# A 941-operation state-space and gated-linear kernel on one core: the hand-written order replaced by another, with 14 bank evacuations on the other engine

## The chip, the cores and the metric

One core of a Trainium2 chip. The number to be judged is the device time of the whole kernel in microseconds (us), as the median of several runs. Engines are called as in the profile: PE is TensorE's matmul, PEld its weight load, DVE is VectorE, ACT is ScalarE, POOL is GpSimd, SP is SyncE, whose queue here only issues DMAs.

## The reference, cut to what matters

```python
xn = _layernorm(x)                                  # x: (1, 2048, 512), bf16
return x + _A_ref(xn, ...) + _B_ref(xn, w_gate, w_up, w_down)

def _A_ref(u, ...):                                 # a state-space layer, N = 128 states
    dB, logdA = dt * Bc, dt * A
    P = jnp.exp(logdA[:, :, None] * l[None, None, :])       # powers, l = 0..2047
    K = jnp.einsum("dn,dnl,dn->dl", Cc, P, dB).real         # one kernel per channel
    y = irfft(rfft(pad(u)) * rfft(pad(K)))[:, :L]           # causal convolution along l
    return y + u * Dskip

def _B_ref(x, w_gate, w_up, w_down):                # F = 1792
    h = _sigmoid(x @ w_gate) * (x @ w_up)
    return h @ w_down
```

## The kernel before, in words

The program first collects 941 small operations in a `_Plan`: each has an engine (or a DMA queue), a function that issues its instructions, the operations that it depends on, and the buffer slots that it takes and gives back. The list `ORDER` is then replayed by `run`. It fixes three things at once: the order of the instructions on every engine, the order of the transfers on every queue (SP's, ACT's, POOL's), and which of the buffers of a pool an operation gets, as the pools are handed out first in, first out. There is nothing dynamic after that. An engine works strictly in its order, so an instruction that waits holds all behind it. The pools that matter: `s` (two pairs of PSUM banks), `gu` (four PSUM banks), `es` (three buffers of the table E), `xx` (three of spectra), `zx`, `kb`, `pp`, `pq`, `vs` (two or more each of the convolution's stages), `hT` (eight of hidden rows), `us` (two of evacuated up rows), `ot` (three of outgoing rows).

The stages, which overlap:

- **Start.** Tiles of x are loaded, normalised (statistics at L547 and L548, the apply at L555 on ACT or L560 on DVE) and transposed on PE (L571) or by DMA (L584). Meanwhile PE runs dummy matmuls (`keep_warm`, L526): 14, 6, 3 and 3.
- **GLU.** Tokens are in four groups of 512, the hidden dimension in 14 tiles of 128. For each: gate matmuls (L1031), sigmoid on ACT (L1043), up matmuls (L1055), product on DVE (L1070). Where the tile's number 14 x group + tile stands in `UEV`, ACT first copies the up bank to `us_sb` (L1066) and DVE multiplies from there; otherwise DVE reads the bank. The down projection (L1099) makes 16 tiles of 128 tokens; tiles 0 to 11 come in between, 12 to 15 at the end.
- **Ladder and tables.** Powers on DVE (L679, L681), squares on ACT (L672), casts on either (L664 on DVE, L666 on ACT, two instructions each). In four chunks DVE then builds table products (L737 to L743 and, with ACT's squares of L790, L795 and L796), and PE multiplies by them (two table matmuls, L821, a selection, L841). The results, copied by ACT, are the kernel's transform.
- **Convolution.** Two sets, p0 and p1, of eight units. Each loads a piece of the transformed input, transforms it on PE (L892), copies the spectrum out of PSUM (L288 on DVE or L290 on ACT), swaps halves (p0: four DMAs on SP; p1: DVE copies, L905), loads a table E (320 KB), makes the kernel's spectrum on PE (L914), multiplies on DVE (L919, L923), transforms back on PE (L936), copies out and stores to `v_scr`. The unit names p0u7 and so on are set and number.
- **Tail.** `v_scr` is read back (SP and ACT queues), closing matmuls (L995, L997), corrections (L955 to L974, which read sums that POOL makes in a block named `pre`, L712 to L716), the last four down tiles, two additions on DVE (L1010 and L1119), the stores.

`ON_DVE` lists operation numbers whose copy, cast or layernorm apply goes to DVE and not to ACT. A number in it is a position in the plan, and each says what it is by its place: 64 to 87 ladder casts, 95 to 124 layernorm applies of tiles 4 to 15, 482, 542, 566 spectrum evacuations of units of p1, 836 to 846 copies of finished down tiles.

Some operation numbers that the steps below speak of: 686 and 688 are the up matmuls and the product of group 1, tile 1; 463 and 464 are the evacuation and the store of p0u6's result; 468 to 471 the four swaps and 475 the first product of p0u7; 349 the first table matmul of the last chunk; 922, 925, 929 and 934 with 936 the down tiles 12 to 15; 840, 848, 762, 754, 676 and 668 closing blocks of the tail; 167 is `pre`; 19 to 22 the dummy matmuls (14, 6, 3, 3).

Of the kernel before, what the change touches and what calls it, by code (L numbers as in the profile page):

```python
# [180 lines left out]
def _consts():  # L181
# [19 lines left out]
    return dict(SR=f(sr), ident=f(np.eye(128)), S1=f(np.tile(S1, (4, 1))), S2=f(np.stack([_build_S2(by), np.roll(_build_S2(by), 32, axis=1)], axis=1)), M2=f(quads(M2[by])), SW=f(sw),  # L201
                MAB=f(np.stack([quads(MA[by], True), quads(MB[by], True)], axis=2)), E=f(_build_E(M2, by).reshape(128, NU // 2, 2, NKT, 128).transpose(1, 0, 2, 3, 4)))

UEV = (3, 5, 8, 9, 10, 11, 15, 16, 17, 18, 19, 20, 21, 23, 24, 26, 27, 28, 29, 30, 31, 32, 33, 34, 35, 36, 37, 38, 39, 40, 41, 42, 43, 44, 45, 54)
ON_DVE = (64, 67, 73, 76, 97, 98, 110, 121, 122, 123, 124, 482, 836, 838)
ON_ACT = (2,)
ORDER = [
# [41 lines left out]

class _Op:  # L250
    __slots__ = ("alt", "tab", "eng", "cost", "fn", "prio", "acq", "rel", "dma", "left", "users", "ready", "start", "done", "seq", "mode")
# [8 lines left out]
class _Plan:  # L260
# [20 lines left out]
    def copy(self, nc, cost, out, in_, *args, **kw):  # L281

        get = lambda v: v() if callable(v) else v
        dve = len(self.ops) in ON_DVE

# [35 lines left out]
def kernel(  # L321
# [214 lines left out]
    def layernorm(i0, i1, prio):  # L536
# [14 lines left out]
        for i in range(i0, i1):  # L551
            dve = i < LN_ACT or len(pl.ops) in ON_DVE
            if not dve:
# [107 lines left out]
    def f_cast(cur, k, dve):  # L661
        for p in range(NP):
            if dve:
                V.tensor_copy(out=W[p][:, k], in_=cur[:, :, DW * p:DW * p + DW])  # L664
            else:
                S.activation(out=W[p][:, k], in_=cur[:, :, DW * p:DW * p + DW], func=ACT.Identity)  # L666
    cast_prev = [None, None]
    for k in range(12):
        cur = wt[(2 * k) % 3]
        sq, nxt = wt[(2 * k + 1) % 3], wt[(2 * k + 2) % 3]  # L670
        if k < 11:
            s_op = pl.add("ACT", 0.95, lambda cur=cur, sq=sq: S.activation(out=sq, in_=cur, func=ACT.Square),  # L672
                          [cur_op] + W_op[-1:], PLAD + k * 0.01)
        dve = len(pl.ops) in ON_DVE
        c_op = pl.add("DVE" if dve else "ACT", 1.04, lambda cur=cur, k=k, dve=dve: f_cast(cur, k, dve), [cur_op],
# [339 lines left out]
    for grp in range(4):  # L1015
        hts, prods = [], []
        for u2 in range(7):
# [4 lines left out]
            for k in (2 * u2, 2 * u2 + 1):  # L1022
# [38 lines left out]
                us = _Slot("us")  # L1061
                on = un in UEV

# [131 lines left out]
```

## Time and profile before

| | |
|---|---|
| runs | 222.93, 221.24, 221.66 us; median 221.66 |
| profiled execution | span 219.8 us, first to last activity, 1.9 below the median of the runs (the only time of that execution that is recorded) |
| busy | PE 209.2 us (95%), DVE 202.2 (92%), ACT 175.9 (80%), POOL 22.6 (10%) |
| transfers | 41.36 MB, 188 GB/s on average |
| chain that ended last, by engine | DVE 48%, PE 41%, DMA 4%, ACT 4%, issue 2% |

The profile lists busy time per engine, the span in 40 slices, the DMA queues, and the chain of work that ended last, followed back from the final instruction to what released each step. Two further views count: groups of instructions of one line and form, with busy time, the mean duration of one in ns, and the idle time before them with what ended it; and the timeline. A busy engine is not always at its peak: matmuls are pipelined, and the durations shown include the overlap with the next.

### The profile page before, as it was taken

How to read it: one execution, taken by the hardware profiler on the slowest of the kernel's cores; microseconds unless marked ns; L12 is line 12 of the kernel's file. 1: busy time of each engine (PE TensorE's matmuls, PEld its weight loads, DVE VectorE, ACT ScalarE, POOL GpSimd, SP SyncE). 2: the span in 40 equal slices, each digit the busy share in tenths (PEclk: the TensorE clock that was granted, in tenths of full speed). 3: DMA queues.
4: the chain of work that ended last, by engine and by line, in shares of the span. 5: the costliest groups of instructions: out<-in, count | busy, mean ns of one | idle time of the engine just before them, and what ended most of it. 6: DMA issues, size and time to landing. Idle time of an engine off the chain costs nothing.

```text
span 219.8 us, 5357 instructions
## 1 busy us (share of the span) xinstructions
PE 209.2 (95%) x2075; PEld 105.0 (48%) x2103; DVE 202.2 (92%) x444; ACT 175.9 (80%) x283; POOL 22.6 (10%) x39
## 2 busy tenths in 40 slices
PE   7999988999999999999999999999989999999994
PEld 2544433444434454445555555554555455543453
DVE  3999999999999999999999999999989999993582
ACT  3699999999999999769899999977578978942000
POOL 2216001001000049100000004000020100000000
PEclk9999999999999999999999999999999999999999
DMA  5997069216667064526818579856857987688743
GB/s 172 333 425 298 7 180 317 80 42 143 237 134 206 18 198 97 202 82 178 244 55 237 152 244 210 212 173 169 228 111 236 265 265 232 189 234 209 220 158 136
DMA packets 40651, 41.36 MB, mean 188 GB/s; under 512 B 9009, under 2 KB 31922, under 8 KB 40498
## 3 DMA queue, kind: packets, MB, share of 16 engines
q1 hardware_dynamic: 39458, 39.12, 57.7%
q0 software_dynamic: 864, 1.57, 4.9%
q10 hardware_dynamic: 304, 0.33, 0.6%
q8 instruction: 16, 0.26, 0.5%
q14 instruction: 9, 0.07, 0.1%
HBM read 25.28 MB, written 12.06 MB: 170 GB/s over the span
## 4 chain that ended last, share of the span: by engine, by line
DVE 48%; PE 41%; DMA 4%; ACT 4%; issue 2%; POOL 0%; DVEq 0%; ACTq 0%
PE bank L1099 11%; DVE big L738 7%; PE pair L914 7%; DVE big L737 6%; PE bank L1031 6%; PE bank L1055 6%; DVE hT_sb L1070 6%; PE pair L936 5%; DVE stats L547 4%; DVE big L742 4%; DVE big L743 3%; DVE big L679 3%; DVE big L681 3%; DMA big<-c_E 3%; ACT big L290 3%; DVE big L613 2%
## 5 line engine op out<-in xcount | busy, mean ns | idle before, releaser
L290 ACT ACTIVATE big<-pair 128x1024 bf16<-128x1024 f32 (+2 forms) x75 | 73.4, 996 | 9.2 <-PE pair L936 1.9
L1055 PE MATMUL bank<-xnT,wu_sb 128*128 128x512 bf16 x214 | 54.4, 379 | 2.5 <-ACT us_sb L1066 1.3
L1031 PE MATMUL bank<-xnT,wg_sb 128*128 128x512 bf16 (+1 forms) x211 | 50.9, 367 | 1.4 <-ACT xnT L576 0.4
L1099 PE MATMUL bank<-wd_sb,hT_sb 128*128 128x512 bf16 (+1 forms) x230 | 50.2, 366 | 0.4
L1043 ACT ACTIVATE hT_sb<-bank 128x512 bf16<-128x512 f32 x52 | 32.1, 643 | 3.8 <-PE bank L1031 3.6
L1031 PEld LDWEIGHTS <-wg_sb 128*128 128x128 bf16 x236 | 21.9, 98 | 26.4 <-issue 5.2
L1099 PEld LDWEIGHTS <-hT_sb 128*128 128x128 bf16 x238 | 22.5, 98 | 24.8 <-issue 2.1
L1055 PEld LDWEIGHTS <-wu_sb 128*128 128x128 bf16 x224 | 21.0, 97 | 27.2 <-issue 5.4
L737 DVE TENSOR_TENSOR big<-big 128x1024 bf16<-128x1024 bf16 (+4 forms) x40 | 26.8, 670 | 0.1
L738 DVE TENSOR_TENSOR big<-big 128x1024 bf16<-128x1024 bf16 (+4 forms) x40 | 26.6, 666 | 0.0
L1066 ACT ACTIVATE us_sb<-bank 128x512 bf16<-128x512 f32 x36 | 22.4, 634 | 0.0
L919 DVE TENSOR_TENSOR big<-big 128x2048 bf16<-128x2048 bf16 x16 | 19.5, 1219 | 0.4
L914 PE MATMUL pair<-big 128*128 128x256 bf16 x160 | 19.8, 272 | 0.1
L914 PEld LDWEIGHTS <-big 128*128 128x128 bf16 x160 | 15.5, 98 | 4.9 <-issue 1.1
L790 ACT ACTIVATE sq_sb<-big 128x256 bf16<-128x256 bf16 (+2 forms) x20 | 13.7, 685 | 3.9 <-DVE big L743 3.8
L743 DVE TENSOR_TENSOR big<-big 128x512 bf16<-128x512 bf16 (+4 forms) x40 | 16.6, 414 | 0.0
L742 DVE TENSOR_TENSOR big<-big 128x512 bf16<-128x512 bf16 (+4 forms) x40 | 16.5, 413 | 0.0
L290 ACT ACTIVATE big<-big 128x256 bf16<-128x256 bf16 x36 | 15.7, 470 | 0.2
L1070 DVE TENSOR_TENSOR hT_sb<-hT_sb,us_sb 128x512 bf16<-128x512 bf16 x36 | 14.9, 421 | 0.0
L905 DVE COPY big<-big 32x1024 bf16<-32x1024 bf16 x32 | 13.5, 421 | 0.5
L1070 DVE TENSOR_TENSOR hT_sb<-hT_sb,bank 128x512 bf16<-128x512 bf16 x20 | 13.2, 684 | 0.5 <-PE bank L1055 0.5
L936 PE MATMUL pair<-big 64*64 64x512 bf16 (+1 forms) x256 | 12.8, 326 | 0.5 <-ACT big L290 0.2
(103 smaller groups left out, 222.2 us busy)
## 6 DMA issues: line engine op xcount, KB each, us to landing
big<-c_E SPq DMA_DIRECT2D x16, 320.0 KB, 4.4
z_scr<-big SPq DMA_DIRECT2D x16, 256.0 KB, 3.0
big<-z_scr SPq DMA_DIRECT2D x16, 256.0 KB, 3.5
v_scr<-big SPq DMA_DIRECT2D x16, 256.0 KB, 2.9
big<-in_A_u_dram SPq DMA_DIRECT2D x4, 512.0 KB, 8.5
big<-big SPq DMA_DIRECT2D x32, 64.0 KB, 3.1
big<-v_scr SPq DMA_DIRECT2D x4, 512.0 KB, 5.0
wu_sb<-in_B_w_up_dram SPq DMA_DIRECT2D x2, 896.0 KB
```

What stands on the lines that cost most here:

```text
L290: nc.scalar.activation(out=get(out), in_=get(in_), func=ACT.Identity)
L737: V.tensor_tensor(out=wide(outp), in0=wide(lo), in1=mre, op=ALU.mult)
L738: V.tensor_tensor(out=wide(tb()), in0=wide(lo), in1=mim, op=ALU.mult)
L742: V.tensor_tensor(out=outp[:, :, 0], in0=outp[:, :, 0], in1=tb()[:, :, 1], op=opr)
L743: V.tensor_tensor(out=outp[:, :, 1], in0=outp[:, :, 1], in1=tb()[:, :, 0], op=opi)
L914: T.matmul(two(sk)[:, o:o + DW], es()[:, g, kt, :], kT[p][:, kt, :], start=kt in (0, NKT - 1), stop=kt >= NKT - 2)
L936: T.matmul(two(sv)[o:o + 64, DW * (2 * g + y):2 * DW * (g + 1)], mab[b:b + 64, 2 * u + g, q, :], pq()[b:b + 64, q, ch] if y else pp()[b:b ...
L1031: T.matmul(bank(sl, k % 2)[:, c0:c1], w_at(w, CUT_G, kt, k), xnT[:, grp, kt, c0:c1], start=(kt == 0), stop=(kt == KT - 1))
L1043: S.activation(out=hT_sb[:, hs.idx, k % 2, :], in_=bank(sl), func=ACT.Sigmoid)
L1055: T.matmul(bank(sl), w_at(wu_sb, CUT_U, kt, k), xnT[:, grp, kt, :], start=(kt == 0), stop=(kt == KT - 1))
L1070: V.tensor_tensor(out=h(), in0=h(), in1=us_sb[:, us.idx, :] if on else bank(sl), op=ALU.mult)
L1099: T.matmul(bank(po)[:, 0:c[1] - c[0]], hT_sb[:, hts[k // 2].idx, k % 2, jj * 128:(jj + 1) * 128], wd_sb[:, k, c[0]:c[1]], start=first and ...
```

## The change

The diff touches three constants. `UEV` goes from 36 to 35 tiles: out 5, 8, 9, 15, 19, 23, 45, in 6, 7, 25, 47, 48, 52. `ON_DVE` goes from 14 to 15: out 64, 67, 73, 76 (casts), 121, 123, 124 (applies), 482 (a spectrum), 836 (a down tile); in 82 (a cast), 95, 96, 108, 109, 111 (applies), 542, 566 (spectra), 844, 846 (down tiles). `ORDER` holds the same 941 numbers in another order. Dependencies, sizes, transfers and buffers are as they were, but which buffer of a pool an operation gets follows the new order. Of the dummy matmuls, the last two groups of three (21, 22) now stand behind the last down tile. The loads of x tiles 4 to 7 come ahead of the first gate weights, and `pre` stands at the end of POOL's queue.

```diff
--- before
+++ after
-UEV = (3, 5, 8, 9, 10, 11, 15, 16, 17, 18, 19, 20, 21, 23, 24, 26, 27, 28, 29, 30, 31, 32, 33, 34, 35, 36, 37, 38, 39, 40, 41, 42, 43, 44, 45, 54)
-ON_DVE = (64, 67, 73, 76, 97, 98, 110, 121, 122, 123, 124, 482, 836, 838)
+UEV = (3, 6, 7, 10, 11, 16, 17, 18, 20, 21, 24, 25, 26, 27, 28, 29, 30, 31, 32, 33, 34, 35, 36, 37, 38, 39, 40, 41, 42, 43, 44, 47, 48, 52, 54,)
+ON_DVE = (82, 95, 96, 97, 98, 108, 109, 110, 111, 122, 542, 566, 838, 844, 846,)
 ON_ACT = (2,)
 ORDER = [
-    1, 24, 0, 23, 2, 34, 25, 27, 4, 3, 6, 26, 33, 35, 37, 28, 36, 29, 30, 38, 43, 44, 46, 39, 40, 45, 10, 7, 13, 19,
-    20, 31, 32, 21, 41, 48, 42, 22, 592, 604, 593, 605, 615, 618, 624, 47, 90, 88, 91, 49, 11, 103, 5, 14, 104, 89,
-    606, 50, 102, 92, 93, 12, 627, 653, 658, 9, 633, 54, 594, 654, 55, 634, 610, 655, 101, 656, 106, 598, 611, 659,
...
-    721, 740, 722, 724, 674, 679, 152, 197, 81, 82, 725, 680, 198, 173, 83, 723, 199, 713, 729, 684, 730, 686, 734,
-    736, 737, 183, 112, 113, 685, 126, 84, 687, 200, 174, 86, 728, 201, 688, 735, 153, 154, 202, 689, 746, 690, 744,
...
-    164, 17, 166, 244, 138, 139, 140, 141, 375, 239, 232, 229, 262, 675, 167, 750, 751, 752, 245, 246, 212, 757, 759,
...
-    786, 769, 784, 286, 385, 293, 362, 828, 829, 463, 822, 790, 443, 823, 444, 276, 287, 386, 803, 279, 420, 440, 294,
-    824, 310, 792, 851, 852, 466, 472, 390, 365, 445, 311, 364, 464, 296, 793, 467, 387, 412, 388, 791, 787, 832, 446,
...
-    301, 363, 471, 366, 468, 405, 772, 370, 314, 474, 831, 771, 773, 302, 304, 319, 303, 305, 853, 856, 427, 394, 371,
-    327, 833, 469, 470, 475, 397, 393, 395, 389, 449, 406, 421, 328, 774, 476, 407, 320, 329, 321, 422, 834, 331, 913,
...
-    348, 424, 410, 430, 540, 845, 431, 349, 351, 838, 350, 352, 432, 565, 836, 433, 901, 404, 409, 906, 902, 415, 416,
...
-    536, 537, 897, 514, 889, 894, 515, 898, 895, 875, 576, 918, 890, 870, 876, 899, 919, 878, 538, 539, 590, 588, 582,
-    581, 577, 860, 578, 877, 591, 585, 579, 920, 900, 879, 880, 922, 840, 848, 925, 841, 842, 584, 849, 923, 926, 676,
-    668, 850, 677, 669, 678, 670, 924, 927, 929, 762, 763, 930, 933, 754, 928, 764, 755, 756, 935, 934, 936, 931, 932,
-    937, 939, 940, 938]
+    0, 1, 19, 2, 3, 4, 23, 10, 24, 6, 7, 25, 26, 33, 34, 27, 13, 11, 28, 5, 29, 43, 30, 8, 31, 35, 9, 20, 44, 37, 36, 45,
+    46, 38, 32, 39, 15, 40, 41, 47, 48, 42, 592, 12, 91, 604, 598, 88, 605, 593, 90, 49, 624, 89, 615, 101, 92, 618, 104,
+    93, 633, 50, 627, 606, 94, 634, 599, 102, 643, 619, 96, 103, 638, 594, 600, 95, 105, 625, 98, 54, 97, 51, 653, 99, 644,
...
+    174, 739, 730, 197, 705, 684, 740, 83, 686, 121, 685, 687, 706, 216, 198, 707, 688, 157, 182, 711, 84, 693, 199, 694,
...
+    294, 296, 772, 392, 420, 469, 770, 297, 463, 295, 473, 445, 771, 464, 298, 468, 398, 831, 446, 393, 474, 299, 470, 802,
+    834, 395, 399, 300, 447, 396, 803, 427, 406, 287, 448, 827, 564, 301, 276, 858, 804, 407, 475, 302, 773, 411, 304, 774,
...
+    326, 308, 343, 341, 843, 344, 342, 317, 345, 414, 346, 402, 333, 493, 403, 845, 516, 347, 494, 404, 334, 348, 415, 349,
...
+    871, 518, 355, 430, 839, 872, 569, 847, 431, 567, 358, 911, 167, 570, 556, 432, 862, 553, 571, 433, 916, 554, 876, 572,
...
+    509, 889, 884, 535, 898, 510, 536, 899, 908, 885, 511, 909, 537, 590, 873, 512, 538, 890, 874, 513, 539, 905, 875, 576,
+    514, 918, 577, 900, 893, 919, 515, 910, 587, 894, 578, 895, 920, 922, 588, 591, 585, 584, 579, 925, 581, 582, 840, 848,
+    841, 935, 923, 926, 849, 842, 762, 933, 924, 850, 754, 927, 929, 928, 763, 755, 764, 676, 756, 930, 677, 668, 934, 669,
+    678, 936, 931, 670, 937, 932, 938, 22, 939, 21, 940,]
```

53 rows, old and new, of the table ORDER are left out of this document.

## The prediction

> **What bounds the kernel now.** I read the page's first two parts, then busy time by stage, the chain that ended last, the groups by form, and last the timeline around the few places where the change could tell.
>
> ```profile
> span 219.8 us, 5357 instructions
> PE 209.2 (95%) x2075; PEld 105.0 (48%) x2103; DVE 202.2 (92%) x444; ACT 175.9 (80%) x283; POOL 22.6 (10%) x39
> ...
> 0.00:10.20 10.20, 8.60 (x42) 3.63 (x43) 6.29 (x23) 5.04 (x9) 2.52 (x12) 1.00 0.74 238
> 10.20:41.50 31.30, 28.88 (x149) 13.31 (x152) 30.61 (x71) 30.95 (x51) 5.38 (x8) 1.00 0.63 231
> 41.50:77.90 36.40, 35.84 (x185) 15.36 (x188) 36.37 (x88) 36.40 (x64) 1.07 (x1) 1.00 0.46 126
> 77.90:100.20 22.30, 22.13 (x303) 10.39 (x309) 22.16 (x55) 19.07 (x35) 8.82 (x9) 1.00 0.52 152
> 100.20:131.20 31.00, 30.30 (x393) 16.74 (x397) 31.00 (x74) 29.77 (x51) 0.36 (x2) 1.00 0.64 187
> 131.20:155.90 24.70, 24.43 (x351) 13.18 (x354) 24.67 (x53) 20.37 (x34) 2.22 (x4) 1.00 0.74 193
> 155.90:199.20 43.30, 41.85 (x558) 23.53 (x565) 40.84 (x75) 33.72 (x43) 2.26 (x3) 1.00 0.79 220
> 199.20:219.80 20.60, 17.15 (x110) 8.83 (x109) 10.23 (x12) 0.59 (x1) 0.00 (x0) 0.99 0.58 177
> ```
>
> Columns of the stages: length, then busy PE, PEld, DVE, ACT, POOL, granted clock, DMA share, GB/s. The cuts are the first gate matmul, the first down tile (41.5), the starts of the four table matmuls (L821), and tile 12 of the down projection (199.2), which opens the tail. The reader is to see that DVE is never free from 41.5 to 155.9 (114.20 of 114.40 us), that ACT is full as well in 41.5–77.9, and that PE and DVE both have about 2 us to spare only in the last long stage. So up to the fourth table matmul **DVE paces**: a wait put into its queue before 155.9 goes to the end whole. After it PE and DVE hand to each other, and the tail is PE's.
>
> **The work itself hardly changes.** The same operations run; fourteen change engine. The price of each:
>
> ```profile
> L1070 DVE TENSOR_TENSOR hT_sb<-hT_sb,us_sb 128x512 bf16<-128x512 bf16 x36 | 14.9, 421 | 0.0
> L1070 DVE TENSOR_TENSOR hT_sb<-hT_sb,bank 128x512 bf16<-128x512 bf16 x20 | 13.2, 684 | 0.5 <-PE bank L1055 0.5
> L1066 ACT ACTIVATE us_sb<-bank 128x512 bf16<-128x512 f32 x36 | 22.4, 634 | 0.0
> L666 ACT ACTIVATE big<-big 128x512 bf16<-128x512 f32 x16 | 9.8, 701 | 0.0
> L555 ACT ACTIVATE big<-big,ln_nb_f,ln_ri_f 128x512 bf16<-128x512 bf16 x5 | 4.2, 883 | 0.0
> L290 ACT ACTIVATE big<-pair 128x1024 bf16<-128x1024 f32 x63 | 64.6, 1044 | 6.3 <-PE pair L936 1.9 <-issue 1.9 <-PE pair L914 1.4
> L288 DVE CAST big<-bank 128x512 bf16<-128x512 f32 x2 | 1.3, 686 | 0.0
> L288 DVE CAST big<-pair 128x1024 bf16<-128x1024 f32 x1 | 1.2, 1225 | 0.0
> ...
> 8.42 0.65 DVE big L560 x2
> 38.91 0.67 DVE big L664 x2
> ```
>
> The last two are pieces of the chain (start, length): two layernorm applies in 0.65, two ladder casts in 0.67. On **DVE**: one product fewer has its up bank evacuated first, 0.684 − 0.421 = +0.26; four casts leave and one comes, two instructions each, 3 × −0.67 = −2.0; three layernorm applies leave and five come, 2 × 0.325 = +0.65; one spectrum evacuation leaves and two come, +1.23; one GLU copy leaves and two come, +0.69. Sum **+0.8 us**. It is not even: casts go from before 80 us, the spectrum and GLU copies come after 156, where DVE gains work worth about 0.9 and had 43.30 − 40.84 = 2.5 free. On ACT: −0.63 + 3 × 2 × 0.65 (a cast is two instructions; 0.701 overlaps a little) − 2 × 0.883 − 1.04 − 0.64 = about −0.2. On PE the sum is the same, but six dummy matmuls of L526 move from the start to after the last down tile.
>
> **The start.**
>
> ```profile
> 1.43 5.92 PE L526 MATMUL bank<-glu_sb 128*128 128x512 bf16 x20 [1.43 <-POOL glu_sb L519]
> ...
> 3.07 0.43 SPq L423 DMA_DIRECT2D wg_sb<-in_B_w_gate_dram  x1
> ...
> 3.96 0.15 PEld L526 LDWEIGHTS <-glu_sb 128*128 128x128 bf16 x1 [0.28 <-issue]
> ...
> 4.38 2.47 PEld L526 LDWEIGHTS <-glu_sb 128*128 128x128 bf16 x12 [0.27 <-issue]
> ...
> 7.49 0.72 PE L571 MATMUL pair<-ident,big 128*128 128x128 bf16 x8
> ...
> 10.20 1.03 PE L1031 MATMUL bank<-xnT,wg_sb 128*128 128x256 bf16 x8
> ```
>
> From 4.38 the weight loads of the dummies follow each other by 2.47 / 12 = 0.21 us (before it, by 0.42: 3.96 to 4.38), so the six are worth 1.3 us, and PE waited for layernorm there anyway. Against it, the load of the first gate weights is issued behind four more tiles of x. I count this even: bounds −1.3 (the dummies did hold PE up) and +0.8 (two issues of 0.43 us ahead of the weights). PE's work ahead of the first down tile is then 34.58 us against 34.66, and I leave 41.5 for it.
>
> With 14 dummies ahead of the first transposes in place of 20, seven at 0.42 and seven at 0.21, PE ends them at 5.8 and pauses 1.6 us to 7.4.
>
> [...]
>
> **41.5 to 77.9: the first new wait.** I added up the back-to-back durations of everything ahead of an instruction on its engine, in the old order and in the new one, and moved the row of the old trace by the difference.
>
> ```profile
> 63.21 1.03 PE L1055 MATMUL bank<-xnT,wu_sb 128*128 128x512 bf16 x4
> ...
> 68.92 1.26 DVE hT_sb L1070 x3
> ```
>
> The first is the up projection of group 1, tile 1; the second, in the chain, begins with its product (first instruction seen at 68.83). The new order has 5.16 us less DVE work ahead of that product, 63.67, but 0.58 more PE work ahead of the matmuls, which then end at 63.21 + 0.58 + 1.03 = 64.82. The product reads the bank itself, so DVE waits **1.2 us**; behind it stand the other products, the ladder and the table products, and ACT's squares wait for those. PE is busy 35.84 of 36.40 here, so it cannot be early. Bounds: 0 if PE comes 1.2 earlier, 1.9 if the +0.8 at the start is also there. I take 1.2.
>
> **100 to 156: the second.** In p0 the halves of a spectrum are swapped by four DMAs on SP's queue.
>
> ```profile
> big<-big SPq DMA_DIRECT2D x32, 64.0 KB, 3.1
> ...
> 118.39 1.03 ACT L290 ACTIVATE big<-pair 128x1024 bf16<-128x1024 f32 x1
> ...
> 131.38 1.14 SPq L423 DMA_DIRECT2D big<-big  x2
> 134.39 1.22 DVE L919 TENSOR_TENSOR big<-big 128x2048 bf16<-128x2048 bf16 x1
> ```
>
> The last row is the first spectrum product of unit p0u7; it moves 2.77 us of DVE work forward, to 131.6. Two of its swaps now stand on SP behind the store of unit 6's result, which waits for ACT's evacuation (the 118.39 row). That moves 7.84 us of ACT work back, to 126.2, and ends at 127.3 (up to 0.9 later if ACT's idle time between does not shrink). Then the store, a swap, another unit's swap and the swap itself, 0.57 us apart by the SP row, so the last is issued at 129.0 and lands 3.1 us later, 132.1 to 133.0, with the queue's own order up to 133.4. DVE waits 0.5 to 1.8 if it comes there unshifted, and nothing if it already carries 1.2 and ACT does not. Bounds 0 and 1.8, taken in the middle, **0.9**.
>
> ```profile
> 81.24 6.26 POOL L714 TENSOR_TENSOR pre<-pre,xnT 128x4 f32<-128x4 f32 x3
> ...
> 171.59 0.86 POOL L1136 DMA_DIRECT2D big<-in_A_u_dram  x1 [10.92 <-ACT big L290]
> ...
> 196.56 0.18 DVE L962 TENSOR_TENSOR rf<-pre,k 128x16 f32<-128x16 f32 x1
> ```
>
> The block `pre` (L712 to L716, these 6.26 us its most) goes to the end of POOL's queue, behind the last accumulating load. That was issued at 171.59 and does not come later in the new order, so `pre` is done by about 181 and read at 196: nothing, unless POOL came 15 us late.
>
> **156 to 199.**
>
> ```profile
> 155.94 1.42 PE L821 MATMUL pair<-big 128*32 128x82 bf16 x128
> ...
> 164.57 2.80 DMA big<-c_E
> ...
> 199.20 3.20 PE L1099 MATMUL bank<-wd_sb,hT_sb 128*128 128x512 bf16 x14
> ...
> 202.99 2.36 DVE L1010 TENSOR_TENSOR big<-pair,big 128x1024 bf16<-128x1024 f32 x2 [3.24 <-PE pair L995]
> ...
> 216.53 0.42 DVE L1119 TENSOR_TENSOR big<-bank,big 128x256 bf16<-128x256 f32 x1 [1.10 <-PE bank L1099]
> ```
>
> PE has 39.95 us of work between its fourth table matmul and tile 12, and takes 43.26. The new order has 0.86 less on PE and 0.9 more on DVE. Both wait for each other here, so I let the stage stand: **0**, bounds −0.9 and +0.9, and −1.65 more if half of PE's 3.3 us of waiting went.
>
> **The tail**, 199.20 to 216.53, is 17.33 us of PE. The new order has one pair of switches fewer between down tiles and closing matmuls (−0.2) but puts four closing blocks together behind tile 13. The last needs the PSUM pair that the second add of L1010 frees (two take 2.36), a wait of some 0.5. The moved dummies end at 216.5 + 1.3 = 217.8, before the last store lands at 219.8. **+0.2**, bounds 0 and +0.6.
>
> Sum: 0 + 1.2 + 0.9 + 0 + 0.2 = +2.3 on a span of 219.8, so 222.1. The runs' median, 221.66, lies 1.9 above the span; with the same 1.9 the time is **224.0 us**, +1.0%.
>
> **Rivals.** (a) *Faster.* No wait forms up to 156, since DVE, ACT and PE shift together; then PE's queue decides, with 0.44 less ahead of the fourth table matmul, 0.86 less between it and tile 12, and half of the 3.3 gone because the E loads on the chain (2.80 at 164.57) are issued earlier: −2.95 + 0.2, so 218.9. For it speaks that PE is the busiest engine; against it, that DVE and not PE paces to 156 and gets work after. It decides once both waits are under 0.3. (b) *Much slower.* The waits add up: 1.2, 1.8, the extra 0.9 of DVE work uncovered, and a third in the last chunk's squares, where DVE's work ahead falls by 0.58 and ACT's rises by 1.23, half of that 1.8: with the tail 5.0, so 226.7. For it speaks DVE's full row, 31.00 of 31.00; against it ACT's 4.3 us of idle in 131–156. [...] (d) *Nothing*: the waits are covered and the stage stands, +0.2, 221.9.
>
> **Chances.** Forecast (222.6 to 225.4) 0.42, a little over half of it above the bound; (a) 0.24, a fifth of it inside 1%; (b) 0.19; (c) 0.03; (d) 0.12. The measurement tells 1%, 2.2 us, from no change: slower 0.23 + 0.19 + 0.03 = 0.45; same 0.19 + 0.05 + 0.12 = 0.36; faster 0.19. The range runs from the middle of (a), 218.8, to past (b), 228.0, and leaves out under 2 in 10.
>
> **What would show it.** DVE idle for over 0.8 us ahead of L1070 at 63–66; idle ahead of L919 at 131–134, released by a swap; the fourth table matmul at 157.3–158.8 (155.9 would kill both waits); 43 ± 1 us from it to tile 12; 17.3–17.9 from there to the last matmul of L1099; DVE busy near 203.0. The forecast is wrong if DVE's row shows no idle tenth before 156, or if the stage after it gives or takes over 1 us.

## The result, and the profile after

The changed kernel is faster: 220.74 us against 222.09 (medians of six runs each), ratio 0.9937 with a 95% interval of 0.9911 to 0.9964, which is −0.6% where +1.0% was forecast. Set against other runs of the kernel before, a second measurement of the changed one gave the same (first experiment).

The changed kernel's page, and its busy time by stage (columns as before; the cuts are the same events at their new times). Its line numbers are 2 lower than before (L1053 is L1055); in experiments whose order list takes fewer lines they are 8 lower, and in `dve_extra` those below the added line are 1 lower.

```profile
span 219.7 us, 5394 instructions
PE 211.9 (96%) x2103; PEld 105.1 (48%) x2103; DVE 202.7 (92%) x442; ACT 174.9 (80%) x284; POOL 18.0 (8%) x39
```

```profile
0.00:10.13 10.13, 7.73 (x36) 3.15 (x37) 6.52 (x23) 5.17 (x9) 2.92 (x12) 1.00 0.72 251
10.13:39.56 29.43, 29.39 (x164) 13.76 (x165) 28.91 (x66) 29.28 (x49) 2.61 (x4) 1.00 0.70 251
39.56:77.78 38.22, 38.11 (x200) 16.45 (x192) 38.01 (x89) 38.15 (x68) 2.79 (x5) 1.00 0.36 99
77.78:100.65 22.87, 22.48 (x300) 10.37 (x301) 22.87 (x60) 20.79 (x38) 1.23 (x3) 1.00 0.69 194
100.65:131.51 30.86, 29.94 (x396) 16.50 (x396) 30.86 (x69) 29.74 (x51) 0.36 (x2) 1.00 0.68 191
131.51:155.05 23.54, 23.54 (x341) 12.22 (x340) 23.27 (x53) 18.38 (x32) 2.12 (x4) 1.00 0.58 151
155.05:198.15 43.10, 41.72 (x562) 23.11 (x561) 41.33 (x75) 32.86 (x42) 5.93 (x9) 1.00 0.80 223
198.15:219.70 21.55, 19.02 (x117) 9.55 (x115) 10.96 (x14) 0.59 (x1) 0.00 (x0) 1.00 0.60 192
```

The reader sees three things. Between the first gate matmul and the first down tile PE now has no idle time (29.39 of 29.43, before 28.88 of 31.30), so that tile starts 2.0 us earlier. The stage from the fourth table matmul to tile 12 is as long as it was (43.10, before 43.26). The last stage is longer (21.55, before 20.60), and the span is the same, 219.7 against 219.8.

**The median gains 1.35 us and this trace shows 0.1 of it.** Two things account for part of the difference. The time outside the span hardly varies for either kernel: 2.10 to 2.23 us in all later runs of the kernel before, 1.75 to 1.85 in those of the changed one. That is 0.35 us of the gain, and no trace shows where it comes from. And the traced execution took 221.50 us, the longest of its six. The spans' medians differ by 0.8 to 1.35 (219.0 against 219.75 to 220.35 in the several sets). The starts of some events in single traces, read from the timelines:

```
                          before  before_again  after  after_again  after_third
first down tile            41.53     41.39      39.56     39.70        39.64
last table product        155.00    154.88     154.52    154.37       154.95
fourth table matmul       155.94    155.80     155.05    154.90       155.47
tile 12                   199.20    198.59     198.15    198.23       197.96
first closing block       202.32    202.32     204.41    204.90       204.11
end of last down matmul   216.49    216.49     216.40    216.33       216.45
time of that execution       -      221.95     221.50    221.44       221.56
```

### The profile page after: what moved, and what is told of

Same layout as the page of the kernel before. It is cut to its first block, busy times and chain, and to the rows that moved or that the text cites. A ratio compares the mean times of both kernels' runs of the same rounds, so it can differ in the third digit from the quotient of the medians.

```text
span 219.7 us, 5394 instructions
## 1 busy us (share of the span) xinstructions
PE 211.9 (96%) x2103; PEld 105.1 (48%) x2103; DVE 202.7 (92%) x442; ACT 174.9 (80%) x284; POOL 18.0 (8%) x39
## 4 chain that ended last, share of the span: by engine, by line
PE 46%; DVE 38%; DMA 8%; issue 3%; ACT 3%; SPq 0%; DVEq 0%; ACTq 0%
PE bank L1053 12%; PE bank L1029 10%; PE bank L1097 10%; DVE big L736 7%; DVE big L735 7%; PE pair L912 5%; DVE big L741 5%; DVE big L740 4%; PE pair L934 3%; DVE hT_sb L1068 3%; DMA v_scr<-big 3%; DVE big L917 3%; DMA big<-c_E 2%; ACT big L288 2%; DMA big<-in_A_u_dram 2%
## 5 line engine op out<-in xcount | busy, mean ns | idle before, releaser
L288 ACT ACTIVATE big<-pair 128x1024 bf16<-128x1024 f32 (+2 forms) x74 | 71.7, 991 | 10.3 <-PE pair L934 3.6
L1053 PE MATMUL bank<-xnT,wu_sb 128*128 128x512 bf16 x224 | 54.2, 380 | 0.2 <-ACT glu_sb L288 0.2
L1097 PE MATMUL bank<-wd_sb,hT_sb 128*128 128x512 bf16 (+1 forms) x238 | 50.8, 367 | 0.0
L1053 PEld LDWEIGHTS <-wu_sb 128*128 128x128 bf16 x224 | 20.5, 98 | 25.7 <-issue 4.3
L1041 ACT ACTIVATE hT_sb<-bank 128x512 bf16<-128x512 f32 x52 | 30.7, 636 | 0.6 <-PE bank L1029 0.5
L1064 ACT ACTIVATE us_sb<-bank 128x512 bf16<-128x512 f32 x35 | 21.6, 626 | 1.1 <-DVE hT_sb L1068 1.0
L788 ACT ACTIVATE sq_sb<-big 128x256 bf16<-128x256 bf16 (+2 forms) x20 | 13.2, 676 | 5.0 <-DVE big L741 4.7
L288 ACT ACTIVATE big<-big 128x256 bf16<-128x256 bf16 x36 | 16.2, 465 | 0.4 <-PE pair L819 0.4
L1068 DVE TENSOR_TENSOR hT_sb<-hT_sb,bank 128x512 bf16<-128x512 bf16 x21 | 13.9, 682 | 0.0
L934 PE MATMUL pair<-big 64*64 64x512 bf16 (+1 forms) x256 | 13.5, 327 | 0.2 <-ACT big L288 0.2
```

What stands on the lines that cost most here:

```text
L288: nc.scalar.activation(out=get(out), in_=get(in_), func=ACT.Identity)
L1041: S.activation(out=hT_sb[:, hs.idx, k % 2, :], in_=bank(sl), func=ACT.Sigmoid)
L1053: T.matmul(bank(sl), w_at(wu_sb, CUT_U, kt, k), xnT[:, grp, kt, :], start=(kt == 0), stop=(kt == KT - 1))
L1068: V.tensor_tensor(out=h(), in0=h(), in1=us_sb[:, us.idx, :] if on else bank(sl), op=ALU.mult)
L1097: T.matmul(bank(po)[:, 0:c[1] - c[0]], hT_sb[:, hts[k // 2].idx, k % 2, jj * 128:(jj + 1) * 128], wd_sb[:, k, c[0]:c[1]], start=first and ...
```

## The experiments

Where a kernel is cut from two orders, the first n operations of one are followed by all others in the order of the second; each operation keeps the engine of the order that it is taken from.

**after_again and before_again.** No edit.

> The changed kernel once more, unchanged, for a second trace of it. Its first trace is of an execution of 221.50 us, 0.76 above the median of its six runs, so part of what that trace shows may belong to that execution alone. Theory S (the gain is made at the start: PE reaches the first down tile 2 us earlier, DVE is 0.5 us ahead and carries this to the fourth table matmul, and the tail gives 0.9 us back): first down tile at 39.6 +- 0.3, fourth table matmul 154.6 to 155.2, tile 12 at 198.0 +- 0.4, tail from there to the last down matmul 18.0 to 18.5, time 220.7. Rival E (the gain is in the tail, and the first trace shows an untypical tail): tail 17.0 to 17.4 in this trace.

> The kernel before once more, for a second trace and for the size of chance: ratio 1.000 within 0.003. In the trace tile 12 at 199.2 +- 0.5 and the tail 17.3 +- 0.2; if the fourth table matmul or tile 12 lies over 0.7 us from the first trace, differences of that size between single traces say nothing.

Measured: 220.84 (0.9936, 0.9911 to 0.9960) and 222.16 (0.9993, 0.9974 to 1.0013). The table shows that the lead at the first down tile, 1.7 to 2.0 us, is the same in all traces, and that tile 12 alone moves by 0.6 between two traces of the kernel before. The end does not follow it: in both the first closing block starts at 202.32. In before_again the view names what it waits for, the last loads of `v_scr`:

```profile
202.32 1.05 PE L995 MATMUL pair<-big 128*64 128x512 bf16 x8 [0.53 <-DMA big<-v_scr]
```

In the first trace tile 12 ends just then and no wait is marked. Tails (tile 12 to the last down matmul) were 17.29 and 17.90 before, 18.25, 18.10 and 18.49 after.

**tail_of_before, tail_of_after.** The order from tile 12 on exchanged.

```diff
 # tail_of_before: changed order up to 922 (tile 12), then
-925, ..., 840, 848, 841, ..., 762, ..., 754, 929, ...   # D13, then four closing blocks, D14
+840, 848, 925, ..., 676, 668, 929, 762, ..., 754, ...   # two closing blocks, D13, two, D14, two
 # tail_of_after: the reverse, behind the order of before
```

> The changed kernel up to tile 12 of the down projection, from there on the order of before (closing blocks split into two groups, dummies still last). Theory S: the tail shrinks from 18.3 to 17.3 us and nothing else moves, 220.7 - 0.9 = 219.8, ratio to before 0.990. Rival E: no faster than the changed kernel, 220.7 or more, as the tail was where its gain came from.

> The kernel before, with the order of the changed one only from tile 12 on. Theory S: the tail costs 0.9 us more, 222.1 + 0.9 = 223.0, ratio 1.004. Rival E: faster than before, 221.0 or less.

Measured: tail_of_before 224.71 (1.0100, 1.0067 to 1.0133), 3.9 slower than the changed kernel; tail_of_after 222.26 (0.9983, 0.9965 to 1.0001), no slower than before. Theory S missed both, by 4.9 and 0.7 us. Rival E's bound holds in the first ("220.7 or more") and misses the second, so neither describes the pair. The timeline of tail_of_before has the reason, above the same place in the changed kernel:

```profile
198.51 3.20 PE L1091 MATMUL bank<-wd_sb,hT_sb 128*128 128x512 bf16 x14
...
204.11 1.05 PE L987 MATMUL pair<-big 128*64 128x512 bf16 x8 [2.40 <-issue]
```

```profile
198.15 6.22 PE L1097 MATMUL bank<-wd_sb,hT_sb 128*128 128x512 bf16 x28
...
204.41 1.05 PE L993 MATMUL pair<-big 128*64 128x512 bf16 x8
...
210.21 4.62 DVE L1008 TENSOR_TENSOR big<-pair,glu_sb 128x1024 bf16<-128x1024 f32 x4 [1.58 <-DMA out_dram<-big]
...
216.44 0.42 DVE L1117 TENSOR_TENSOR big<-bank,big 128x256 bf16<-128x256 f32 x1 [0.68 <-PE bank L1097]
```

With one down tile as cover, PE stands idle 2.40 us until 204.1. The view names no releaser ("issue"). ACT's queue issues loads of `v_scr` from 200.03 on, 4.1 us earlier, and in before_again such loads are what the view names ahead of this block (0.53 us, row above), so it is most likely these that PE waits for. With tiles 12 and 13 first (x28) the same work covers the wait. The changed order issues these loads 2.0 us after tile 12 has started (200.16), where the first trace of before had issued them 0.1 us ahead of it (199.11), so its tail has to hide more; of the tails tried, the changed one does it best, and its length is no loss that could be had back. The trace shows 1.9 of the 3.9 us (223.37). In the other five executions the mean granted clock is 0.992 and the times are longer still; the last section shows what 0.992 came from in two traces. Two views of one trace, "tail 0.9 us longer" and "last closing block can't start before 204", look alike until they are tested apart.

**Where along the kernel the gain is made.**

```diff
 start_of_after:       first 300 operations of after (to ~68 us), then before
 start_of_before:      first 300 of before, then after
 through_3_of_after:   first 705 of after (to the fourth table matmul), then before
 through_3_of_before:  first 690 of before, then after
```

> The order and the engines of the changed kernel for its first 300 operations (to about 68 us, with the six dummies last as there), the rest in the order of before. Theory S (the gain is made at the start): the first down tile at 39.6, the fourth table matmul 0.4 to 0.9 us earlier than before and with it the end, 222.2 - 0.7 = 221.5, ratio 0.997. Rival L (the gain is made from the fourth table matmul on, where tile 13 hides the last loads of v_scr and the adds come later): no gain, 222.2, ratio 0.999 to 1.001.

> The kernel before for its first 300 operations, then the order of the changed one, so the start alone is undone (the six dummies are back at the start). Theory S: first down tile at 41.4, DVE 0.5 us late from there, 220.8 + 0.7 = 221.5, ratio 0.997. Rival L: nothing lost, 220.8, ratio 0.994.

> The changed kernel up to just before its fourth table matmul (705 operations, six dummies last), then the order of before. Theory S: the whole gain, 222.2 - 1.4 = 220.8 or a little less, as the longer tail is not there. Rival L: 222.2, ratio 0.999 to 1.001.

> The kernel before up to just before its fourth table matmul (690 operations), then the order of the changed one. Theory S: fourth table matmul at 155.9 as before, nothing gained, the tail 0.9 longer: 222.2 to 222.8. Rival L: the whole gain, 220.8, ratio 0.994.

Measured: 224.09 (1.0112, 1.0078 to 1.0146), 225.75 (1.0171, 1.0149 to 1.0194), 221.46 (0.9980, 0.9957 to 1.0002), 223.61 (1.0076, 1.0056 to 1.0096). Three of the four are slower than either parent, and neither theory said so. New waits of 1 to 2 us stand behind the seam (at 72 to 79 us in start_of_after and start_of_before, at 151 in through_3_of_before). These rows are from the waits of PE or DVE in the three, in this order:

```profile
PE pair L813 <- DVE big L734: 2.1, 1, 2.1
PE pair L690 <- ACT big L282: 1.9, 1, 1.9
```

```profile
DVE hT_sb L1062 <- ACT us_sb L1058: 1.7, 1, 1.7
DVE hT_sb L1062 <- PE bank L1047: 1.2, 1, 1.2
```

```profile
PE bank L1091 <- ACT us_sb L1058: 1.7, 1, 1.7
```

In start_of_after all six executions also have a mean clock of 0.992. So these three say nothing on where the gain lies. Only through_3_of_after has a quiet seam: tile 12 at 198.83, last down matmul ending at 216.22, and at most 0.5 us of the gain. With tail_of_after's 0.2 to 0.4, about half of it comes only when the whole order is there, if the parts add up; which step makes that half isn't shown.

**pe_late.** Is it PE's lead that keeps the forecast wait away?

```diff
-            for r in range(2):
+            for r in list(range(2)) * (7 if i0 == 6 else 1):   # forward transform at ~26 us, same values again
```

> The changed kernel, with the forward transform of tiles 6 and 7 (8 matmuls at about 26 us, just before the first down tile is due) issued seven times over, which writes the same values: 6 x 0.354 = 2.1 us of PE work that put PE back to where it stood in the kernel before (first down tile 41.6). Theory W (the wait that was forecast at 64 us did not come only because PE was 2 us ahead): DVE now waits 0.8 to 1.2 us for the up matmuls of group 1, tile 1, the fourth table matmul comes 1 us later and the time is 220.8 + 1.0 = 221.8. Rival N (PE's place does not matter there, the order leaves room anyway): no wait over 0.3 us before L1068 around 64, time 220.8 +- 0.3.

Measured: 222.55 (1.0024, 1.0000 to 1.0047), 1.7 slower than the changed kernel. The 48 more matmuls cost less than I had put down (56 in 1.72 us), so PE came 1.1 later to the first down tile, 40.66.

```profile
26.01 1.72 PE L696 MATMUL pair<-big 32*64 32x512 bf16 x56
...
29.60 0.69 DVE L1068 TENSOR_TENSOR hT_sb<-hT_sb,bank 128x512 bf16<-128x512 bf16 x1 [0.95 <-PE bank L1053]
```

DVE waits for an up tile as theory W says, but at 29.6 and not at 64: from there DVE is as late as PE and no wait forms at 64. The delay reaches the end (last table product 0.5 later than the mean of three traces, tile 12 by 1.4, last down matmul by 1.0). PE's place matters; the place of the wait was wrong. As only 1.1 of the 2.0 us were given back, a wait at 64 with none of the lead is not tested.

**dummies_back, no_end_dummies.**

```diff
 dummies_back:   order 19, 20, tr, 21, tr, 22, first gate matmul, as before; none at the end
 no_end_dummies:
-            for _ in range(n):
+            for _ in range(n if n > 3 else 0):
```

> The changed kernel with the dummy matmuls of L526 where they stood before: 20 ahead of the first transposes, 3 between, 3 ahead of the first gate matmul, none at the end. Theory G (PE's 2 us come from the gate and up order of the first group, whose banks come free in time; PE waits for layernorm ahead of the first gate matmul anyway): first down tile at 39.6 to 40.0, time 220.8 to 221.0. Rival D (they come from the dummies): first down tile at 40.9, and as in pe_late a wait at 64, 221.4.

> The changed kernel without the six dummy matmuls that stand last (they write a bank that nothing reads). Theory G (they run beside the last stores and cost nothing, and the time outside the span, 1.8 us against 2.15 of the kernel before, does not come from them): 220.7 +- 0.3, outside the span 1.8. Rival X (the end dummies are the reason why less time lies outside the span): outside 2.1, time 221.0 to 221.1.

Measured: 221.08 (0.9961, 0.9933 to 0.9988), first down tile at 39.76; and 220.63 (0.9935, 0.9911 to 0.9959), 1.81 us outside the span. Theory G holds in both: the dummies are neither the 2 us of PE nor the time outside the span.

**flags_of_before, flags_of_after.** The order kept, the engines exchanged.

```diff
 flags_of_before (changed order):   ON_DVE = the 14 numbers of before
 flags_of_after (order of before):  ON_DVE = the 15 numbers of after
```

> The changed order, with the engines of before for casts, layernorm applies, spectrum and down evacuations (the 35 up tiles stay as changed). By the rows: before the fourth table matmul DVE gets 2.0 us of casts more and 0.65 us of applies less, +1.35, after it 1.9 less. Theory P (DVE paces to 155, so work put on it goes to the end): fourth table matmul at 156.3, time 220.8 + 1.35 = 222.2, less what the lighter last stage gives. Rival O (the order alone makes the gain, and the swap of engines is neutral): 220.8 +- 0.3.

> The order of before, with the changed kernel's engines for casts, applies, spectrum and down evacuations (the 36 up tiles stay as before). Theory P: 1.35 us less DVE work before the fourth table matmul, 154.6 in place of 155.9, but 1.9 more after it with 2.5 free: 222.2 - 1.35 + 0.5 = 221.4. Rival A (ACT is full from 20 to 78 us, and three casts of 1.29 less two applies of 0.88 put 2.1 us more on it, which comes back to DVE as a wait): fourth table matmul at 156 or later, 222.2 to 224.

Measured: 226.35 (1.0202, 1.0177 to 1.0227) and 231.78 (1.0433, 1.0412 to 1.0455). Theory P's sums were 4 and 10 us too small, and rival A, right in its direction, 8. The waits of DVE in the first, and of DVE and PE in the second:

```profile
DVE hT_sb L1062 <- ACT us_sb L1058: 1.9, 2, 1.6
```

```profile
DVE big L673 <- ACT big L664: 4.0, 4, 1.7
...
DVE big L787 <- ACT sq_sb L782: 2.5, 1, 2.5
```

```profile
PE bank L1047 <- DVE hT_sb L1062: 2.7, 1, 2.7
```

In the order of before with four more casts on ACT, DVE waits 4.0 us for ACT's ladder squares (L664), in place of the 2.0 that it saved. That the casts are what delays the squares is likely, but they were not moved by themselves. The granted clock also fell once in the traced execution of flags_of_after, to 0.50 at 36 to 38 us (last section). Which engine evacuates is worth under 1 us as a sum of durations and 5 to 10 us when the order isn't made for it.

**loads_of_after.**

```diff
 first 45 operations of after (loads, statistics, first transposes), then before; dummies as before
```

> The kernel before with the first 45 operations (first loads, statistics, first two transposes) in the changed order, the dummies where they stood before. Theory S1 (DVE's 0.5 us come from the earlier first statistics, 2.97 against 3.36, and go through DVE to the fourth table matmul and to the end): last table product 154.5, time 222.0 - 0.4 = 221.6, ratio 0.998. Rival S0 (the first load just varies by that much): 222.0, ratio 0.999 to 1.001, last table product 154.9 to 155.0.

Measured: 223.47 (1.0058, 1.0033 to 1.0083); neither theory. The waits of PE and of DVE:

```profile
PE bank L1047 <- DMA wu_sb<-in_B_w_up_dram: 2.4, 1, 2.4
```

```profile
DVE hT_sb L1062 <- PE bank L1047: 1.8, 2, 1.3
```

The order of before starts its up projections with tiles 12 and 8, the changed one with tiles 6, 3, 0 and 2. Tiles 12 and 8 need the second half of the up weights, whose load the new order puts later. This load order does not fit the old matmul order. Rival S0 is right in one point: DVE waits 2.9 us for its first statistics here, but also in before_again, with the old load order, and 3.4 in after_again, with the new one. The first load just varies by that much.

**store_buffer, tail_new4, after_third.**

```diff
-    pl = _Plan(dict(... ot=3 ...))
+    pl = _Plan(dict(... ot=4 ...))          # the fourth lies where the spectra were
 tail_new4, besides:
-D12 D13 s2 s2 ... s2 ... s2 D14 s2 ... s2 D15 D15
+D12 D13 s2 s2 ... D14 s2 s2 ... D15 s2 s2 D15
```

> The changed kernel with a fourth buffer for outgoing rows, so that the third addition of L1008 need not wait until a store has landed (1.58 us in the first trace of the changed kernel, 0.87 in the second, 0.60 in pe_late, none in dummies_back). Theory T (in the changed tail the landing of stores sets the end, and its variation is the difference between traces and medians): no wait of L1008 on out_dram, tail from tile 12 to the last down matmul 17.6 to 17.9 in place of 18.1 to 18.25, time 220.2 to 220.5. Rival V (the last loads of v_scr set it, the adds have room): tail as before, 220.8.

> As store_buffer, and in the tail tile 14 is moved ahead of the second pair of closing blocks, and half of tile 15 ahead of the third pair. Theory T: PE no longer waits for PSUM pairs between tiles 13 and 15, tail 17.3 to 17.6, last add at 216.0, time 219.9 to 220.3, the fastest so far. Rival Q (the adds, six of 1.18 us and eight of L1117, now end last): last add at 216.5 or later, 220.8 or more.

> The changed kernel once more, for a third trace: tile 12 at 198.2 +- 0.3; the start of the first closing block is the landing of the last v_scr load (204.41 and 204.90 so far) or the end of tile 13, 204.3, whichever is later; the wait of the third addition 0.5 to 1.6. If the time is 220.5 or less, the tail in it shows what the faster executions have.

Measured: 220.70 (0.9940, 0.9915 to 0.9965); 222.02 (0.9996, 0.9976 to 1.0015); 221.56 (one execution). With the fourth buffer the third add starts right behind the others,

```profile
208.74 2.34 DVE L1008 TENSOR_TENSOR big<-pair,glu_sb 128x1024 bf16<-128x1024 f32 x2
```

where it had waited to 210.21, and the time is the same, 220.70 against 220.84. In the first trace the chain that ended last does run through the store (2.65 us), yet without the wait the last down tile starts at 213.01 in place of 213.17: so little hung on it, and theory T falls. tail_new4 is rival Q: its last adds begin at 216.39, three in 1.34 us, where PE had ended at 216.15. In after_third the first closing block comes right behind tile 13, as expected, and the third addition waits 1.88 us, longer than expected. No version beats the changed kernel by more than the noise. What does differ between executions of the changed tail is the second pair of closing blocks, whose first matmuls wait for `v_scr` in after_third (first row; 221.56 us) and in no_end_dummies (second row; 222.44), but not in dve_extra (third row; 220.95, the shortest traced):

```profile
207.47 0.62 PE L993 MATMUL pair<-big 128*64 128x512 bf16 x4 [1.23 <-DMA big<-v_scr]
```

```profile
208.37 0.62 PE L993 MATMUL pair<-big 128*64 128x512 bf16 x4 [1.33 <-DMA big<-v_scr]
```

```profile
206.04 0.62 PE L994 MATMUL pair<-big 128*64 128x512 bf16 x4
```

That the faster executions are those in which these loads land in time fits these three. But in the first two traces of the changed kernel only the weight loads waited for them, 0.39 and 0.53 us, with at most 0.25 of idle PE, and they took 221.5 all the same. It isn't shown.

**dve_extra.**

```diff
-            def fpa(kb=kb, pp=pp, xx=xx):
+            def fpa(kb=kb, pp=pp, xx=xx, n=2 if (p, u) == (0, 1) else 1):
+              for _ in range(n):
```

> The changed kernel with the first spectrum product of unit p0u1 (L917, at about 112 us) computed twice, 1.14 us more on DVE and nothing else. Theory C (DVE paces until the fourth table matmul, and what is put on it before goes to the end whole): last table product and fourth table matmul 1.1 us later, 155.6 and 156.1, time 220.7 + 1.1 = 221.8. Rival M (from 100 us on PE or ACT decide and DVE has room): under 0.4 of it at tile 12, 221.0 or less.

Measured: 221.59 (0.9980, 0.9960 to 1.0000), 0.75 to 0.85 slower than the two medians of the changed kernel and 0.96 slower than no_end_dummies, which was measured beside it. That is near the 1.1 of theory C. The trace says less: the last table product at 155.10 (154.37 to 154.95 without), the fourth table matmul at 155.63, and tile 12 at 197.96, not later at all. It is the shortest of the twelve executions. By the median the 1.14 us go to the end, by this one trace they are gone at tile 12; that stays undecided.

## Why the prediction was wrong, step by step

- **The start: "I leave 41.5 for it"** is the step that failed first, and the wait at 64 us was built on it. PE's work ahead of the first down tile hardly changed, as worked out (busy 37.1 us up to it, before 37.5), but I carried over the idle time of the old trace: 4.0 us before, 2.4 now, so the tile came at 39.56. The rows of the up matmuls for 10.3 to 41.4, before and after:

```profile
L1055 PE MATMUL bank<-xnT,wu_sb 128*128 128x512 bf16 x58 | 14.5, 378 | 1.8 <-ACT us_sb L1066 1.3 <-DVE hT_sb L1070 0.4
```

```profile
L1053 PE MATMUL bank<-xnT,wu_sb 128*128 128x512 bf16 x64 | 15.0, 380 | 0.0
```

  In the old order PE waited 1.8 us here for banks that ACT and DVE had not freed. In the new one it waits for none. The view that would have told it stood in the profile of before: I quoted 28.88 of 31.30 and did not ask what the 2.4 us of idle time waited for. I priced the waits that a new order could bring and not those of the old order that it takes away.
- **The wait at 64 us (+1.2)** is 0. The up tile starts at 61.53 in place of the 63.79 worked out and ends at 62.56; DVE reaches its product at 63.35 (63.67). Had the tile come 2.26 us later, as worked out, DVE would have waited:

```profile
61.53 1.89 PE L1053 MATMUL bank<-xnT,wu_sb 128*128 128x512 bf16 x8
...
63.35 0.68 DVE L1068 TENSOR_TENSOR hT_sb<-hT_sb,bank 128x512 bf16<-128x512 bf16 x1
```

- **The wait for swaps (+0.9)** is 0, and this is the second step that failed. The store came at 125.90, 1.4 us ahead of the time worked out. Of the five swaps behind it the third is, by the order, the unit's last; it was issued at 127.6 (worked out: 129.0) and landed 2.0 us later, not 3.1. That is 129.6, and the product started at 130.88 (131.6) with 1.3 us to spare.

```profile
125.90 0.37 SPq L421 DMA_DIRECT2D v_scr<-big  x1
126.32 3.17 SPq L421 DMA_DIRECT2D big<-big  x5
...
130.88 1.21 DVE L917 TENSOR_TENSOR big<-big 128x2048 bf16<-128x2048 bf16 x1
```

  These two waits are 2.1 of the +2.3. The lower bound of both, 0, was the right end. The 14 dummies ran to 6.42 and the first transposes began at 6.70, so the pause was 0.28 us and not 1.6. No run shows the loss of clock at the start to which (c) gives 0.03 of the chances: the granted clock is 1.00 in the first two stages, before and after, and with a pause of 0.28 us it wasn't put to the test.
- **The work itself (+0.8 on DVE)** came out at +0.5 (202.2 to 202.7), on ACT at −1.0 in place of −0.2. The prediction and the title count fourteen operations that change engine; the lists move nineteen between ACT and DVE, nine leaving DVE and ten coming, and the sum prices all of them.
- **DVE's start**, counted even, was rightly even as far as single traces tell: the 0.4 us at the first statistics is chance (loads_of_after), and the last table product came between 0.1 later and 0.6 earlier.
- **156 to 199 (0)** was right: 43.10, 43.33 and 42.49, against 43.26 and 42.79.
- **The tail (+0.2)** was undersized in the traces, 18.1 to 18.5 against 17.3 to 17.9. But tile 12 was the wrong place to measure it from: when the last loads of `v_scr` land counts as well (0.53 us of waiting in before_again, most likely 2.40 in tail_of_before), and the last down matmul ended within 0.2 us of before.
- **Span to time (+1.9)** was taken as one number for both kernels; it is 2.15 before and 1.80 after.

Case (a) had the direction and the condition: no wait up to 156. Its size, 218.9, was too far, since nothing was gained after 156; the 3.3 us of waiting that it halves there are 1.45 by PE's busy row of before (41.85 of 43.30). What stays open: which step makes the larger part of the gain, as the 2 us won at the start are down to 0.3 to 1.0 at the fourth table matmul and to 0.0 to 0.2 at the last down matmul of the traces; what makes the 0.35 us outside the span (it is 1.96 in through_3_of_after, and both 1.75 and 2.17 occur within flags_of_before), and the 0.7 us or so by which the untraced executions of the changed kernel are shorter than its traced ones.

## What to carry to other kernels

When an order changes, take the old trace's idle time apart by its releasers before carrying it over: the waits that the old order had are as much part of the change as those that the new one may bring. A list of engines, an order of loads and an order of work are tuned together, so exchanging one of them by itself cost up to 4% here while its sum of durations changed by under 1%. And a single trace does not resolve half a per cent: compare several, and compare the time outside the span as well.

## What the runs showed of the hardware

TensorE's granted clock fell in two traces, each time behind waits of PE. In start_of_after PE waited 1.92 and 2.06 us, until 75.07 and 79.38, with 2.2 us of work between; in flags_of_after one wait of 2.7 us (PE's row above) ended at 34.6. Then (columns as above, the clock is the third from the right; start_of_after first):

```profile
82.00:84.00 2.00, 2.00 (x6) 0.65 (x6) 1.12 (x4) 1.23 (x4) 1.63 (x5) 0.52 0.12 16
```

```profile
36.00:38.00 2.00, 1.78 (x5) 0.69 (x5) 2.00 (x5) 1.48 (x2) 0.00 (x0) 0.50 0.94 394
```

The clock is about half in those stretches (0.52 and 0.50) and the mean over the span 0.992 in both traces. In flags_of_after it is 0.86 as a mean of 33 to 36 us, 0.50 from 36 to 38, 0.85 from 38 to 40 and 1.00 from 40 to 44; in start_of_after 1.00 from 70 to 80, 0.63 from 80 to 82, 0.52 from 82 to 84 and 1.00 from 84 to 90. What it falls short of 1.00 by, times the length, is 0.42 + 1.00 + 0.30 = 1.7 us in the first and 0.74 + 0.96 = 1.7 us in the second. That by itself takes the mean over 222 to 230 us down to 0.992, and it is at most what one such fall costs (an estimate from these means). So the untraced executions of tail_of_before and start_of_after at 0.992 may each hold one; no trace shows it. A wait of 2.4 us in loads_of_after (PE's row above, between 18 and 24 us) brought no fall: the clock is 1.00 in every stretch from 0 to 36 us. Nor did the one of 2.40 us in tail_of_before (until 204.1), where the mean of the traced execution is 1.0. So in these traces the length of one pause alone does not decide.
